# Second layer of the last two blocks of an attention and channel-mixing kernel: four of its seven products grow in one PSUM place, by token halves

## The chip, the cores and the metric

The kernel runs on one core of a Trainium2 chip. The metric is the device time of one execution in microseconds (us). Three runs of the kernel before took 336.69 to 336.91 us, with a median of 336.83 us. The profile shows one further execution, which took 336.81 us; the span from its first to its last instruction is 335.1 us.

The engines are named as in the profile: PE (TensorE, matrix products), DVE (VectorE), ACT (ScalarE), POOL (GpSimd) and SP (SyncE, which here only issues DMAs). The name of an engine with a q behind it (DVEq) is its sequencer, which waits on semaphores, branches and issues DMAs.

## The reference

An attention with extra "beacon" keys, then a token mix of low rank, then two dense layers over channels with a residual:

```python
scores = scale * np.matmul(q, k_all.transpose(0, 1, 3, 2))     # 8 batches, 8 heads, 576 queries, 592 keys, D = 64
a = np.exp(scores - max);  a /= a.sum(-1, keepdims=True) + 1e-09
x = np.matmul(a, v_all)                                        # then heads side by side: 8 x 576 x 512
u = x + (x.transpose(0, 2, 1) @ U @ V).transpose(0, 2, 1)      # token mix, rank 32
out = u + np.maximum(u @ w_ch1, 0.0) @ w_ch2                   # 512 -> 2048 -> 512 channels
```

The inputs and the output are float32. The kernel keeps operands of matrix products in float16 and sums in float32.

## The kernel before

All 4608 rows of the mixed tokens are cut into nine blocks of 512 tokens. Block 0 is computed plainly. Blocks 1 to 8 come from `fast_units`, which returns a list of small units; the main program takes them from one queue, in order, and puts attention work between them while there is any. Engine queues are in order, and the order of the program is kept, so the order of the units is the order on each engine. The last two blocks, 7 and 8 (`QUADS`), run when attention is nearly over; for them `quads` is true, and for block 8 `last` is true as well.

A block's first layer leaves g, the 2048 hidden values of 512 tokens, in the tile gT. The second layer multiplies g by w2 with seven products instead of eight (a scheme of Strassen's kind). g is cut by hidden half and token half into a11, a12 (first 256 tokens) and a21, a22 (last 256); VectorE makes four sums of these (`sums`, line 624):

- S1 = a21 + a22, S2 = S1 - a11, S3 = a11 - a21, S4 = a12 - S2.

The matching combinations of w2 (wt) are made once. The products, with the letter of their PSUM tile:

- M1 = a11 b11 (A), M2 = a12 b21 (F), M6 = S2 t2 (B), M7 = S3 t3 (C), M5 = S1 t1 (D, fresh), M4 = a22 t4 (E), M3 = S4 b22 (D, added to M5).

The four quarters of the output, each 256 tokens by 256 channels, are then

- out11 = M1 + M2, out12 = M1 + M6 + M5 + M3, out21 = M1 + M6 + M7 + M4, out22 = M1 + M6 + M7 + M5,

plus the residual u, which lies token-major in the float16 tile ut. A product is two halves of 128 tokens; a half is 8 matmuls of 256 columns into [128, 256] float32. For the block marked `last`, the second half of D is cut again into two of 128 columns.

Before the change a product's PSUM tile [128, 2, 256] holds both halves, and `after(k)` deals with it when both are done. ScalarE copies M1 to SBUF as s1 (line 800). VectorE adds F + s1 (out11), B + s1 (u2 = M1 + M6) and C + u2 (u3), each 128x512 (line 782). In blocks 7 and 8 GpSimd adds the residual to u2 for out12 before the D sums are there, and in block 8 also to u3 for out22; out11 and out21 get theirs from GpSimd after VectorE's add (`residual`). In block 8 the order is A, F, B, C, E, D, D, since lines 842 and 843 swap M4 ahead of M5; in block 7 it is A, F, B, C, D, E, D. `after_g` (line 746) says after which unit a piece of a sum is issued to VectorE.

`store` issues the DMA to HBM. In block 7 a store is put on SP's queue a few units later. In block 8 it is issued at once: out11 and out21 whole (256 KB) on SP, out22 whole on ACT, out12 in three pieces (128 KB and 64 KB on SP, 64 KB on ACT).

The end of the program is a conditional: a register says whether the general version has to run, which it does not on these inputs. The register is loaded 12 units before the end, a hint for the branch (line 1508 in the profile) stands 5 units before the end, and each engine reaches the branch (line 1463) when its last unit has been issued. Behind the branch an engine has a few semaphore instructions, and SP then waits for every DMA and every engine; a barrier over the engines closes the program. All sequencers read their instructions from memory, with DMAs that the profile calls kind instruction.

Of the kernel before, what the change touches and what calls it, by code (L numbers as in the profile page):

```python
# [11 lines left out]
F32 = mybir.dt.float32  # L12
I32 = mybir.dt.int32
AF = mybir.ActivationFunctionType
# [4 lines left out]
P = 128  # L19
# [11 lines left out]
def kernel(  # L31
# [13 lines left out]
    nc = tc.nc  # L45
    B, H, S, D = q.shape
# [5 lines left out]
    NDC = FF // P  # L52
    NH2 = H // 2
    E = D + 1
# [45 lines left out]
    small = ctx.enter_context(tc.tile_pool(name="small", bufs=2))  # L100
# [70 lines left out]
    HF, HC, HT = NDC // 2, DM // 2, 256  # L171
# [423 lines left out]
    def fast_units(t0, dst, last=False, quads=False):  # L595
# [21 lines left out]
        def sums(i, d0, n):  # L617
            a11, a12, a21, a22 = cell["a"]
            s1, s2, s3, s4 = cell["s"]
            o, x, y, op = [  # L620
                (s1, a21, a22, ALU.add), (s2, s1, a11, ALU.subtract),
                (s3, a11, a21, ALU.subtract), (s4, a12, s2, ALU.subtract),
            ][i]
            nc.vector.tensor_tensor(out=o[:, ds(d0, n)], in0=x[:, ds(d0, n)], in1=y[:, ds(d0, n)], op=op)  # L624
# [118 lines left out]

            return [lambda k=k, slot=slot: unit(k, slot) for k, slot in enumerate(slots)]

        after_g = {0: ((0, 6, 2), (1, 6, 2)), 1: ((2, 0, 4),), 2: ((2, 4, 4),), 7: ((3, 0, 4),), 8: ((3, 4, 4),)}
        sums_at = after_g if quads else {k - NDC: x for k, x in SUMS.items()}

        b11, b21, b22 = w2[:, 0:HF, 0:HC], w2[:, HF:NDC, 0:HC], w2[:, HF:NDC, HC:DM]
        t1, t2, t3, t4 = (wt[:, i, :, :] for i in range(4))  # L750

        def pieces(bank):
            return [(0, 0, HC), (1, 0, P), (1, P, P)] if last and bank == "D" else [(0, 0, HC), (1, 0, HC)]

        def product(bank, a, bm, fresh, i, c0, w):
            key = (bank, i, c0) if last and bank == "D" else bank
            if key not in banks:
                banks[key] = pst([P, w] if key != bank else [P, 2, HC], F32, name="mps" + bank)
            ps = banks[key] if key != bank else banks[key][:, i, :]
            for d in range(HF):  # L760
                nc.tensor.matmul(  # L761
                    ps, a()[:, d, ds(P * i, P)], bm[:, d, ds(c0, w)],
                    start=fresh and d == 0 and (i == 0 or key != bank), stop=d == HF - 1, skip_group_check=True,
                )

        def freed(bank):
            for key in [k for k in banks if k == bank or k[0] == bank]:
                emptying(banks.pop(key))
# [12 lines left out]
        def add(out, x, y, eng=nc.vector):  # L781
            eng.tensor_tensor(out=out, in0=x, in1=y, op=ALU.add)  # L782

        def store(name, h, c, i=None, c0=0, w=HC):
            if i is None:
                both = dst(2 * h, 2 * P)[:, ds(HC * c, HC)].rearrange("(k p) c -> p k c", p=P)
                eng = nc.scalar if last and name == "22" else nc.sync
                u = lambda t=obs[name]: eng.dma_start(out=both, in_=t)
                storing.append([2, u]) if not last else u()
            else:  # L790
                eng = nc.scalar if i and not c0 else nc.sync
                eng.dma_start(out=dst(2 * h + i, P)[:, ds(HC * c + c0, w)], in_=obs[name][:, i, ds(c0, w)])

        def residual(name, h, c):
            add(obs[name], obs[name], u_of(h, c), nc.gpsimd)
            store(name, h, c)

        def after(k):
            if k == 0:
                nc.scalar.activation(out=kept("s1"), in_=banks["A"], func=AF.Copy)  # L800
                freed("A")
            elif k == 1:
                add(out_tile("11"), banks["F"], cell["s1"])
                freed("F")
                residual("11", 0, 0)
            elif k == 2:
                add(kept("u2"), banks["B"], cell["s1"])
                freed("B")
                if quads:
                    add(out_tile("12"), cell["u2"], u_of(0, 1), nc.gpsimd)  # L810
            elif k == 3:
                add(kept("u3"), banks["C"], cell["u2"])
                freed("C")
                if last:
                    add(out_tile("22"), cell["u3"], u_of(1, 1), nc.gpsimd)
            elif products[k][0] == "E":
# [3 lines left out]
            elif products[k][3] and not last:  # L820
                add(out_tile("22"), banks["D"], cell["u3"])
                residual("22", 1, 1)
            elif not last:
                add(obs["12"] if quads else out_tile("12"), banks["D"], obs["12"] if quads else cell["u2"])
                freed("D")
                if quads:
                    store("12", 0, 1)
                else:
                    residual("12", 0, 1)

        def a_of(i):
            return lambda: cell["a"][i]
# [9 lines left out]
        if last:  # L842
            products[4:6] = products[5:3:-1]

        def c_unit(k, j):
            bank = products[k][0]
            p = pieces(bank)[j]
            product(*products[k], *p)
            late = quads and k == 3
            for x in () if late else sums_at.get(2 * k + j, ()):  # L850
                sums(*x)
            if bank == "D" and last:
                i, c0, w = p
                o = obs["22" if products[k][3] else "12"][:, i, ds(c0, w)]
                add(o, banks["D", i, c0], o)
                if k == 6:
                    store("12", 0, 1, i, c0, w)
                    emptying(banks.pop(("D", i, c0)))
                elif j == len(pieces(bank)) - 1:
                    store("22", 1, 1)  # L860
            elif j == len(pieces(bank)) - 1:
                after(k)
            for x in sums_at.get(2 * k + j, ()) if late else ():
                sums(*x)

        units = g_quads() if quads else [lambda k=k: g_unit(k) for k in range(NDC)]
# [157 lines left out]
    first = []  # L1024
# [488 lines left out]
```

## Time and profile before

| what | value |
|---|---|
| median of 3 runs | 336.83 us (336.69 to 336.91) |
| the profiled execution, whole | 336.81 us |
| its span | 335.1 us |
| PE busy, share of the span | 326.1 us, 97% |
| DVE, ACT, POOL busy | 249.8, 190.5, 156.2 us |
| mean granted PE clock | 0.997 of full speed |
| second layer of block 7 on PE | from 291.75 us on |
| second layer of block 8 on PE | from 316.80 us on |
| last compute instruction | DVE, from 329.62 us on |

A page's numbers are those of one execution. A line of the timeline names its start, its length, engine, line of the code, operation, output and inputs by the program's names, shape and count, and in brackets the idle time before it and what ended it. Times of PE rows are of pipelined matmuls whose ends are modelled: rows of neighbouring products overlap a little, so the pace is read from one row's end to the next one's.

### The profile page before, as it was taken

Reading aid. Unit: us, or ns where it says so; the run is one execution under the profiler, and the core shown is the slowest. Engines: PE = TensorE matmul, PEld = TensorE weight load, DVE = VectorE, ACT = ScalarE, POOL = GpSimd, SP = SyncE. Lnnn points to the kernel's source line nnn. Section 1 sums busy time; section 2 is a strip of 40 time slices with the busy share of each in tenths; the row PEclk is TensorE's granted clock in tenths of the full one; section 3 lists DMA queues with packets and bytes.
Section 4 is the critical chain, followed back from the end, with each engine's and each line's share of the span. In section 5 each row is a group of like instructions: output and inputs, shape, how many; then the busy total and the mean of one; then the engine's idle time right before and its main releaser. Section 6 shows DMA issues by size and latency. Waiting matters only on the chain.

```text
span 335.1 us, 9084 instructions
## 1 busy us (share of the span) xinstructions
PE 326.1 (97%) x3614; PEld 223.5 (67%) x3614; DVE 249.8 (75%) x564; ACT 190.5 (57%) x411; POOL 156.2 (47%) x191
## 2 busy tenths in 40 slices
PE   8899999999999999999999999999999999999992
PEld 3565655555577656865687888755875588788792
DVE  6676888678897768765876677677777978786782
ACT  5957951788973677167735784469445404604600
POOL 8988815764336540687067805160497014022041
PEclk9999999999999999999999999999999999999998
DMA  7999999999999994999999997974113514104113
GB/s 158 149 180 166 177 205 188 206 185 140 67 149 146 132 179 80 147 183 170 162 101 182 149 126 115 123 157 87 51 33 103 86 43 125 33 32 129 30 35 103
DMA packets 150530, 41.99 MB, mean 125 GB/s; under 512 B 131280, under 2 KB 149904, under 8 KB 150480
## 3 DMA queue, kind: packets, MB, share of 16 engines
q0 software_dynamic: 87568, 18.18, 71.9%
q1 hardware_dynamic: 62272, 22.54, 37.1%
q8 instruction: 30, 0.49, 0.6%
q10 hardware_dynamic: 640, 0.62, 0.6%
q14 instruction: 20, 0.16, 0.2%
HBM read 37.45 MB, written 9.44 MB: 140 GB/s over the span
## 4 chain that ended last, share of the span: by engine, by line
PE 89%; DVE 3%; POOL 2%; ACT 2%; DMA 2%; issue 1%; DVEq 0%; POOLq 0%
PE gps L635 24%; PE po L427 9%; PE mpsD L761 8%; PE sps L409 6%; PE mpsF L761 4%; PE cps L913 4%; PE mpsC L761 4%; PE mpsB L761 4%; PE mpsA L761 4%; PE gps L887 4%; PE mpsE L761 4%; PE qpsA L674 3%; PE gps L663 2%; DMA vs<-in_v_dram 2%; PE qpsD L674 2%; PE sps L370 1%
## 5 line engine op out<-in xcount | busy, mean ns | idle before, releaser
L418 ACT ACTIVATE expt<-sps 128x496 f16<-128x496 f32 (+2 forms) x192 | 82.1, 544 | 41.6 <-PE sps L409 41.6
L782 POOL TENSOR_TENSOR ob<-ob,ut 128x512 f32<-128x512 f32 x29 | 35.1, 1211 | 129.3 <-DVE ob L782 120.5
L761 PEld LDWEIGHTS <-gT 128*128 128x128 f16 x912 | 85.4, 98 | 13.4 <-issue 3.1
L635 PE MATMUL gps<-uT,w 128*128 128x512 f16 (+1 forms) x448 | 91.9, 349 | 0.2 <-ACT kT L1039 0.2
L635 PEld LDWEIGHTS <-w 128*128 128x128 f16 x448 | 40.4, 98 | 31.9 <-issue 2.5
L646 ACT ACTIVATE gT<-gps 128x512 f16<-128x512 f32 x72 | 42.8, 617 | 25.2 <-PE gps L635 19.9
L624 DVE TENSOR_TENSOR gT<-gT 128x1024 f16<-128x1024 f16 (+3 forms) x90 | 46.7, 542 | 1.0
L240 POOL DMA_DIRECT2D vs<-in_v_dram x50 | 39.7, 807 | 13.1 <-DMA w<-in_moe_w_ch_dram 10.7
L427 PEld LDWEIGHTS <-expt 128*128 128x128 f16 x900 | 33.8, 98 | 10.0 <-issue 1.8
L427 PE MATMUL po<-vs,expt 128*128 128x65 f16 x900 | 36.5, 194 | 0.4 <-DMA vs<-in_v_dram 0.2
L348 DVE TENSOR_TENSOR expt<-expt,bigmask 128x768 f16<-128x768 f16 x54 | 35.3, 694 | 1.4 <-ACT expt L418 1.2
L436 DVE TENSOR_TENSOR xb<-po,rec 128x320 f16<-128x320 f32 x64 | 31.5, 492 | 2.2
L435 DVE RECIPROCAL rec<-po 128x5 f32<-128x5 f32 x64 | 12.1, 189 | 19.4 <-PE po L427 19.0
L644 DVE TENSOR_SCALAR gT<-gps 128x512 f16<-128x512 f32 x24 | 16.5, 689 | 13.0 <-PE gps L635 12.4
L686 ACT ACTIVATE lk<-qpsA 128x512 f32<-128x512 f32 x18 | 10.3, 598 | 25.3 <-PE qpsA L674 25.3
L409 PE MATMUL sps<-qT,kT 64*128 64x80 f16 (+4 forms) x288 | 22.6, 281 | 0.0
L376 ACT ACTIVATE expt<-sps 128x496 f16<-128x496 f32 (+2 forms) x48 | 20.4, 565 | 0.6 <-PE sps L370 0.6
L986 POOL DMA_DIRECT2D st<-in_q_dram x20 | 17.0, 870 | 7.4 <-DMA qT<-st 6.9
L409 PEld LDWEIGHTS <-kT 64*128 64x128 f16 x288 | 10.2, 94 | 12.8 <-issue 8.2
L986 POOL DMA_DIRECT2D st<-in_k_dram x20 | 16.9, 856 | 1.6 <-DMA st<-in_q_dram 1.6
L761 PE MATMUL mpsE<-wt,gT 128*128 128x256 f16 x128 | 16.3, 273 | 0.0
L887 PE MATMUL gps<-uT,w 128*128 128x512 f16 x64 | 16.2, 379 | 0.1
(145 smaller groups left out, 463.5 us busy)
## 6 DMA issues: line engine op xcount, KB each, us to landing
out_dram<-ob SPq DMA_DIRECT2D x34, 256.0 KB, 3.0
vs<-in_v_dram POOLq DMA_DIRECT2D x18, 128.0 KB, 6.7
w<-in_moe_w_ch_dram POOLq DMA_DIRECT2D x4, 512.0 KB, 6.3
w<-in_moe_w_ch_dram POOLq DMA_DIRECT2D x2, 1024.0 KB, 12.8
st<-in_k_dram POOLq DMA_DIRECT2D x12, 128.0 KB, 6.6
st<-in_q_dram POOLq DMA_DIRECT2D x12, 128.0 KB, 7.1
st<-in_k_dram POOLq DMA_DIRECT2D x4, 288.0 KB, 11.8
st<-in_q_dram POOLq DMA_DIRECT2D x4, 288.0 KB, 12.7
```

Source lines behind the costliest of these rows:

```text
L240: nc.gpsimd.dma_start(out=dst[a : a + nq[j], j, :, :], in_=src[hs, ds(q0[j], nq[j]), :].rearrange("h p d -> p h d"))
L348: nc.vector.tensor_tensor(out=e, in0=e, in1=bigmask[:, :, :].rearrange("p (a b) x -> p a b x", b=2), op=ALU.min)
L409: nc.tensor.matmul(banks[i][:, ds(at0 + o, w)], kT(hp, c, ch), qT[hp, c, ds(qa, w)], start=True, stop=True, skip_group_check=len(unit) > 1,)
L418: nc.scalar.activation(out=at[p][3][i][:, ds(AT[g], gw[g])], in_=bank[:, ds(at0, gw[g])], func=AF.Exp, scale=scale)
L427: nc.tensor.matmul(po[:, j, :], ex[0 : nk[c], ds(blk[(c, j)], P)], vs[0 : nk[c], ds(c * H * E + h * E, E)], start=(c == 0), stop=(c == j),)
L436: nc.vector.tensor_tensor(out=xb[:, :, ds(h * D, D)], in0=po[:, :, 0:D], in1=r.broadcast_to([P, NT, D]), op=ALU.mult)
L624: nc.vector.tensor_tensor(out=o[:, ds(d0, n)], in0=x[:, ds(d0, n)], in1=y[:, ds(d0, n)], op=op)
L635: nc.tensor.matmul(g[:, ds(o, w)], w1[:, cc, ts(dc, P)], uT[:, cc, ds(at, w)], start=(cc == 0 and o == 0), stop=(cc == NCC - 1), skip_grou ...
L646: nc.scalar.activation(out=cell["g"][:, dc, :], in_=g, func=AF.Relu)
L761: nc.tensor.matmul(ps, a()[:, d, ds(P * i, P)], bm[:, d, ds(c0, w)], start=fresh and d == 0 and (i == 0 or key != bank), stop=d == HF - 1, ...
L782: eng.tensor_tensor(out=out, in0=x, in1=y, op=ALU.add)
L986: coming.append(lambda d=dst, s=src, a=m[j] - nq[j], n=m[j], j=j: nc.gpsimd.dma_start(out=d[a:n, j, :, :], in_=s[:, ds(q0[j], nq[j]), :].r ...
```

## The change

It concerns blocks 7 and 8 alone. A new function `chain_units` replaces `c_unit` there:

- M1, M6, M7 and M4 are accumulated into the same PSUM tile, one tile of [128, 256] for each token half (name "A"). Between two of them the tile is read: ScalarE copies half by half after M1 (s1, for out11), VectorE adds it to the residual after M6 (out12), after M7 (out22) and after M4 (out21). VectorE thus reads ut itself, and the tiles u2 and u3 are gone, and with them GpSimd's adds for out12, out22 and out21. Only out11 keeps GpSimd's.
- The order in both blocks is A, F, B, D, C, E, D (M1, M2, M6, M5, M7, M4, M3). M5 has its own tiles, by half (and in block 8 by three pieces, as before). VectorE adds M5 to out22 right after M7's half, and M5 + M3 to out12 at the end.
- The pieces of S3 and S4 are issued at other units: the second half of S3 after the first half of M6 instead of before M2, the two of S4 after the first two pieces of M5.
- In block 8 out22 and out21 are stored by halves of 128 KB: out22's first half on SP and its second on ACT, out21's both on ACT. In block 7 stores are as before.

The numbers of units (14 for block 7, 16 for block 8) are the same, so that the branch hint and the register's load stand at the same unit counts.

```diff
-        after_g = {0: ((0, 6, 2), (1, 6, 2)), 1: ((2, 0, 4),), 2: ((2, 4, 4),), 7: ((3, 0, 4),), 8: ((3, 4, 4),)}
-        sums_at = after_g if quads else {k - NDC: x for k, x in SUMS.items()}
+        after_g = {0: ((0, 6, 2), (1, 6, 2)), 1: ((2, 0, 4),), 4: ((2, 4, 4),), 6: ((3, 0, 4),), 7: ((3, 4, 4),)}
+        sums_at = {k - NDC: x for k, x in SUMS.items()}
...
-                eng = nc.scalar if i and not c0 else nc.sync
+                eng = nc.scalar if name == "21" or i and not c0 else nc.sync
                 eng.dma_start(out=dst(2 * h + i, P)[:, ds(HC * c + c0, w)], in_=obs[name][:, i, ds(c0, w)])
...
-        if last:
-            products[4:6] = products[5:3:-1]
...
+        def chain_units():
+
+            halves = [(0, 0, HC), (1, 0, HC)]
+            small = [(0, 0, HC), (1, 0, P), (1, P, P)] if last else halves
+
+            def grown(k, name, i, c0, w):
+                _, a, bm, _ = products[k]
+                fresh = (name, i, c0) not in banks
+                if fresh:
+                    banks[name, i, c0] = pst([P, w], F32, name="mps" + name)
+                ps = banks[name, i, c0]
+                for d in range(HF):
+                    nc.tensor.matmul(
+                        ps, a()[:, d, ds(P * i, P)], bm[:, d, ds(c0, w)],
+                        start=fresh and d == 0, stop=d == HF - 1, skip_group_check=True,
+                    )
+                return ps
+
+            def first(i, c0, w):
+                ps = grown(0, "A", i, c0, w)
+                if i == 0:
+                    kept("s1")
+                nc.scalar.activation(out=cell["s1"][:, i, :], in_=ps, func=AF.Copy)
+
+            def second(i, c0, w):
+                product(*products[1], i, c0, w)
+                if i:
+                    after(1)
+
+            def begun(k, name, h, c, i, c0, w):
+                ps = grown(k, "A", i, c0, w)
+                if i == 0:
+                    out_tile(name)
+                add(obs[name][:, i, :], ps, u_of(h, c)[:, i, :])
+
+            def ended(name, i, c0, w):
+                o = obs[name][:, i, ds(c0, w)]
                 add(o, banks["D", i, c0], o)
...
+            def sent(name, h, c, i, c0, w):
+                if last:
+                    store(name, h, c, i, c0, w)
+                elif i:
+                    store(name, h, c)
+
+            def third(i, c0, w):
+                begun(3, "22", 1, 1, i, c0, w)
+                for p in small:
+                    if p[0] == i:
+                        ended("22", *p)
+                sent("22", 1, 1, i, c0, w)
+
+            def fourth(i, c0, w):
+                begun(5, "21", 1, 0, i, c0, w)
+                sent("21", 1, 0, i, c0, w)
+                freed(("A", i, c0))
+
+            def fifth(*p):
+                grown(6, "D", *p)
+                ended("12", *p)
+                sent("12", 0, 1, *p)
+                freed(("D", p[0], p[1]))
+
+            steps = [(first, halves), (second, halves), (lambda *p: begun(2, "12", 0, 1, *p), halves)]
+            steps += [(lambda *p: grown(4, "D", *p), small), (third, halves), (fourth, halves), (fifth, small)]
+            us = [lambda f=f, p=p: f(*p) for f, ps in steps for p in ps]
+
+            def unit(n, u):
+                u()
+                for x in after_g.get(n, ()):
+                    sums(*x)
+
+            return [lambda n=n, u=u: unit(n, u) for n, u in enumerate(us)]
+
+        if quads:
+            return g_quads() + chain_units()
```

More of the change, by code (lines that the diff above doesn't have):

```diff
@@ L819, in after @@
                 residual("21", 1, 0)
[L820 to L824, printed above, removed]
+            else:
+                add(out_tile("12"), banks["D"], cell["u2"])
                 freed("D")
[L826 to L829, printed above, removed]
+                residual("12", 0, 1)
         def a_of(i):
@@ L848, in c_unit @@
             product(*products[k], *p)
-            late = quads and k == 3
-            for x in () if late else sums_at.get(2 * k + j, ()):
+            for x in sums_at.get(2 * k + j, ()):
                 sums(*x)
-            if bank == "D" and last:
-                i, c0, w = p
-                o = obs["22" if products[k][3] else "12"][:, i, ds(c0, w)]
-                add(o, banks["D", i, c0], o)
[L856 to L862, printed above, removed]
```

32 lines of the change are left out of this document (14 added, 18 removed).

## The prediction

> **What bounds the kernel now.** I read the page first, for where time can be lost at all.
>
> ```profile
> span 335.1 us, 9084 instructions
> ## 1 busy us (share of the span) xinstructions
> PE 326.1 (97%) x3614; PEld 223.5 (67%) x3614; DVE 249.8 (75%) x564; ACT 190.5 (57%) x411; POOL 156.2 (47%) x191
> ```
>
> TensorE is busy for 97% of the span and the change leaves it the same matmuls, so only its gaps and the stretch behind its last matmul can move. Next, the chain in order of time, of which these are the first and last of the seven products of block 7:
>
> ```profile
> 291.75 1.75 PE mpsA L761 x16
> ...
> 302.43 1.75 PE mpsD L761 x16
> ```
>
> From 291.75 to 302.43 + 1.75 = 304.18 us stand seven products at 1.75 us and one tiny matmul: no gap, nothing to win in block 7, something to lose. Then the timelines of TensorE, VectorE and GpSimd for block 8:
>
> ```profile
> 321.87 1.91 PE L761 MATMUL mpsC<-wt,gT 128*128 128x256 f16 x16
> 323.62 1.91 PE L761 MATMUL mpsE<-wt,gT 128*128 128x256 f16 x16
> 325.37 1.93 PE L761 MATMUL mpsD<-wt,gT 128*128 128x256 f16 x24
> 327.65 1.93 PE L761 MATMUL mpsD<-w,gT 128*128 128x256 f16 x24 [0.36 <-DVE ob L782]
> ```
>
> ```profile
> 321.32 0.68 DVE L782 TENSOR_TENSOR ob<-mpsF,kept 128x512 f32<-128x512 f32 x1
> 322.07 0.69 DVE L782 TENSOR_TENSOR kept<-mpsB,kept 128x512 f32<-128x512 f32 x1
> 323.82 0.69 DVE L782 TENSOR_TENSOR kept<-mpsC,kept 128x512 f32<-128x512 f32 x1 [1.05 <-PE mpsC L761]
> 324.43 2.24 DVE L624 TENSOR_TENSOR gT<-gT 128x1024 f16<-128x1024 f16 x2
> 326.59 0.68 DVE L782 TENSOR_TENSOR ob<-mpsE,kept 128x512 f32<-128x512 f32 x1
> 327.19 0.80 DVE L782 TENSOR_TENSOR ob<-mpsD,ob 128x256 f32<-128x256 f32 x3
> 328.73 0.74 DVE L782 TENSOR_TENSOR ob<-mpsD,ob 128x256 f32<-128x256 f32 x2 [0.73 <-PE mpsD L761]
> 329.62 0.29 DVE L782 TENSOR_TENSOR ob<-mpsD,ob 128x128 f32<-128x128 f32 x1 [0.15 <-PE mpsD L761]
> ```
>
> ```profile
> 322.13 1.16 POOL L782 TENSOR_TENSOR ob<-ob,ut 128x512 f32<-128x512 f32 x1 [17.69 <-DVE ob L782]
> 323.25 1.16 POOL L782 TENSOR_TENSOR ob<-kept,ut 128x512 f32<-128x512 f32 x1
> 324.64 1.48 POOL L782 TENSOR_TENSOR ob<-kept,ut 128x512 f32<-128x512 f32 x1 [0.23 <-POOL ob L782]
> 327.35 1.15 POOL L782 TENSOR_TENSOR ob<-ob,ut 128x512 f32<-128x512 f32 x1 [1.23 <-DVE ob L782]
> ```
>
> TensorE has one gap in block 8, 0.36 us ahead of M3. M3 grows in the tile that VectorE must first read for out22, and VectorE comes late: its two sums of S4 take 2.24 us together, beside GpSimd's add at 324.64. Alone they cost 0.7 us each:
>
> ```profile
> L624 DVE TENSOR_TENSOR gT<-gT 128x1024 f16<-128x1024 f16 x2 | 1.3, 685 | 0.0
> ```
>
> The last arithmetic ends at 329.62 + 0.29 = 329.91 us, and the span at 335.1: 5.2 us of tail. The busy times by stretch (the last two columns are the DMA engines' busy share and GB/s) and the issues (KB each, us to landing; the last row is the last store) tell what it is:
>
> ```profile
> 329.00:330.00 1.00, 0.58 (x11) 0.41 (x8) 0.74 (x3) 0.00 (x0) 0.00 (x0) 1.00 0.99 325
> 330.00:331.00 1.00, 0.00 (x0) 0.00 (x0) 0.00 (x0) 0.00 (x0) 0.00 (x0) 1.00 1.04 334
> 331.00:332.00 1.00, 0.00 (x0) 0.00 (x0) 0.00 (x0) 0.00 (x0) 0.00 (x0) 1.00 0.57 139
> 332.00:333.00 1.00, 0.00 (x0) 0.00 (x0) 0.00 (x0) 0.00 (x0) 0.00 (x0) 1.00 0.19 40
> ```
>
> ```profile
> out_dram<-ob SPq DMA_DIRECT2D x1, 64.0 KB, 3.9
> ```
>
> From 329 us the DMA engines are full for two and a half microseconds. out22 (ready at about 328), out21 (ready when GpSimd ends, 327.35 + 1.15 = 328.5) and out12 go out together, 768 KB; at 330 GB/s that is 2.3 us. The last 64 KB land 3.9 us after their issue, at about 333.8. A 256 KB store with nothing beside it, the one issued at 323.3, needs:
>
> ```profile
> DMA to landing us min/median/max: 2.2/2.2/2.2
> ```
>
> A second thing ends as late. These are the branch at the end and the first instruction behind it, by sequencer:
>
> ```profile
> L1463 POOLq EVENT_SEMAPHORE  x5: 17/42/43, 330.0 to 330.3; - x5
> ...
> L1463 POOLq COMPARE_BRANCH  x1: 63/63/63, 327.4 to 327.4; - x1
> ...
> L1463 DVEq COMPARE_BRANCH  x1: 90/90/90, 329.6 to 329.6; - x1
> L1463 ACTq COMPARE_BRANCH  x1: 68/68/68, 329.9 to 329.9; - x1
> ...
> L1463 ACTq EVENT_SEMAPHORE  x1: 17/17/17, 331.6 to 331.6; - x1
> L1463 DVEq EVENT_SEMAPHORE  x1: 21/21/21, 333.9 to 333.9; - x1
> ```
>
> VectorE's sequencer goes on only at 333.9, 4.3 us after its branch; GpSimd's took 2.6 us (327.4 to 330.0), ScalarE's 1.7. VectorE's instructions seem to be fetched through the same full DMA engines. So two paths reach the end: last landing 333.8 and 1.3 us, or VectorE's resumption 333.9 and 1.2 us.
>
> **The change, part by part.**
>
> *TensorE's order.* A half is 1.75 / 2 = 0.87 us. C ends at 321.87 + 1.91 = 323.78, so A ended at 318.53, F at 320.28, B at 322.03. In the new order M5 ends at 323.78, M7's halves at 324.66 and 325.53, M4's at 326.40 and 327.28, M3 at 327.28 + 1.93 = 329.21, if TensorE never waits: 0.36 us earlier than 329.58.
>
> *VectorE, step by step.* M2's add (0.68) stands behind one sum of S3 less, so it starts at 320.7 instead of 321.3 and GpSimd's residual of out11 runs from about 321.5 to 322.7. A 128x256 add costs
>
> ```profile
> L782 DVE TENSOR_TENSOR ob<-mpsD,ob 128x256 f32<-128x256 f32 x2 | 0.8, 416 | 0.7 <-PE mpsD L761 0.7
> ```
>
> 0.42 us. M6's first half is read 321.33 to 321.75. Then comes the moved half of S3, while GpSimd runs. The pair at 324.43 shows the price: it ended at 326.67, 0.55 after GpSimd's add (324.64 + 1.48 = 326.12). So I let S3 wait for GpSimd and end at 322.7 + 0.55 = 323.25; without that it would be 322.4. M7 begins at 323.78: cover 0.5 us. M6's second half is read by 323.7, and the two sums of S4, with GpSimd idle, at 0.6 us from start to start, end at about 324.9. M7's first half (324.66) is read 324.9 to 325.3 and M5 added to it by 325.7; M4's first half may enter that tile from 325.53, cover 0.2 us. M7's second half is read 325.7 to 326.1, M4's second half needs it at 326.40, cover 0.3. M3 needs M5's tiles read by 325.7 (first half) at 327.28: where 0.36 us were lost, 1.5 are spare. M4's adds follow at 326.7 and 327.3, M3's at 328.2, 328.6 and 329.26, the last 0.29 long: VectorE ends at 329.55 against 329.91, so **-0.36 us**. The covers of 0.2 and 0.3 are thin; beyond them each 0.1 us of VectorE's lateness is 0.1 us of TensorE's. Nothing excludes 0.5 us there; I take none, as every duration in the list is a measured one.
>
> *GpSimd* loses three adds (1.16, 1.48, 1.15): off the path by themselves. *ScalarE* copies M1 by halves, with 1.75 us of M2 as cover. It issues out22's second half and both of out21, behind which only its 64 KB of out12 wait: the issues fall at about 326.6, 326.9 and 327.8, that of out12 at 328.9. SP issues out22's first half at 325.6, then out12 at 328.65 and 329.58.
>
> *Block 7.* The same order has covers of 0.6 us (S3 before M7) and some 0.3 us (M4 into M7's tile). No gap there before, none expected: 0.
>
> *The stores.* out22 goes out 1.5 to 2.5 us earlier, out21 about 1 to 1.5. Behind 328.6 us only out12's 256 KB are left, 0.8 us at 330 GB/s, and the last 64 KB are issued when the 128 before them are nearly through. Landing after issue: from 2.2 (the lone 256 KB) to 3.9 (today); I take 2.4, near the lone row since the queue in front is gone. The Trainium skill, "DMA: Bandwidth & Descriptors", section "Latency and other measured facts", gives 0.2 us on average and 2 us at high load for an access to HBM, the largest part of a DMA's fixed cost; by that alone the whole excess of 1.7 us would be load and the time 0.2 lower.
>
> *VectorE's sequencer.* Branch at 329.6 - 0.36 = 329.25. From branch to going on: 1.7 (ScalarE's row) to 4.3 (its own, DMA engines full). GpSimd's 2.6 was with them nearly idle; I take 3.0, close to that, for a third of the traffic.
>
> **Sum.** By the landing: 329.58 + 2.4 + 1.3 = 333.3. By VectorE's sequencer: 329.25 + 3.0 + 1.2 = 333.45. The later decides: a span of 333.4, and with 336.81 - 335.1 = 1.7 around it **335.1 us**, 1.7 us or 0.5% under the profiled 336.81 (which is 0.02 under the median). Lower end: landing 1.6 (below 2.2, for a quarter of its bytes) gives 332.5, ScalarE's 1.7 gives 332.15, so 334.1. Upper end of this case, with 3.9 in the landing's place or a stall of 0.5: 335.9.
>
> **Rivals.**
>
> 1. *The tail is not the stores' load.* VectorE's sequencer takes its 4.3 us whatever else moves. Then 329.25 + 4.3 + 1.2 = 334.75, and **336.4 us**: the same within 0.2%, about what a measurement of this kernel can tell from no change. For it: GpSimd's fetch was slow with idle engines too. Against: ScalarE's and GpSimd's were both far shorter.
> 2. *A code fetch sits in front of the last store.* In 330.3 to 330.6 us one instruction packet kept a DMA engine:
>
> ```profile
> q8 instruction: 1, 0.02, 23.2%
> ```
>
> 23.2% of 16 engines for 0.3 us is 1.1 us of one. A store waits for its slowest engine: 2.2 + 1.1 = 3.3 us, end 329.58 + 3.3 + 1.3 = 334.2, **335.9 us**. For it: after 332 us the DMA engines still work at a share of 0.19, a few stragglers. The Trainium skill, same page, section "Queues, rings and completion order", says each DMA engine takes turns between queues by whole packets, so a packet of code holds up the data behind it; the straggling share agrees.
> 3. *Slower: in-place growth ties TensorE to VectorE.* Each of M6, M7 and M4 must wait, half by half, until the tile is read. There are 3 x 2 x 2 = 12 such handovers; were each fully exposed at 0.42 us, TensorE would lose 5.0 us, **340.2**; with half of them 337.6. It decides once more than four are exposed (1.7 / 0.42). For it: covers of 0.2 to 0.3 us in four of them a block at most. Against: the halves alternate, and between M1, M6 and M7 stands a product of 1.75 us.
>
> **How the numbers follow.** The likeliest case, 335.1 (334.1 to 335.9), has 0.60, and 0.04 lies below it. Rival 2 has 0.15, rival 1 has 0.13, rival 3 has 0.08. Faster by over 0.2% (below 336.16): 0.60 + 0.04 + 0.15 = 0.79; within 0.2%: 0.13; slower: 0.08. The range reaches to rival 1: 334.1 to 336.5, leaving 0.04 below and 0.08 above.
>
> **What would show it.** Right: no idle time before M3; the 128x1024 sums of S4 at 0.7 us; DVE's last add 0.3 to 0.4 us earlier than 329.91; the DMA share under 0.9 from 330 us on, the last store landing in 2.2 to 3 us, VectorE's first instruction behind the branch before 333. Wrong: TensorE waiting for VectorE at mpsA's third or fourth product, in block 7 above all; a last landing still near 3.9; or a resumption of VectorE 4 us behind its branch, which would leave little more than the 0.36.

## The result, and the profile after

The changed kernel takes **335.65 us** (median of 8 runs, 335.21 to 336.39) against 336.76 us (336.39 to 337.13, 8 runs) of the kernel before, run beside it: a ratio of **0.9968, 95% interval 0.9957 to 0.998**. It is faster by 1.1 us or 0.3%. The forecast was 335.1 (334.1 to 336.5). The profiled execution took 336.39 us with a span of 334.5 us. It is the slowest of the eight, 0.74 us above their median, so the profile shows less gain than the median.

The head of the page, to set beside that of before:

```profile
span 334.5 us, 9085 instructions
PE 326.3 (98%) x3614; PEld 223.9 (67%) x3614; DVE 251.7 (75%) x572; ACT 190.8 (57%) x413; POOL 148.5 (44%) x185
```

The timelines of TensorE, VectorE and GpSimd in block 8 (start, length, engine, line, operation; in brackets the idle time before it):

```profile
316.90 1.91 PE L854 MATMUL mpsA<-w,gT 128*128 128x256 f16 x16
...
323.90 3.66 PE L854 MATMUL mpsA<-wt,gT 128*128 128x256 f16 x32
327.40 1.93 PE L854 MATMUL mpsD<-w,gT 128*128 128x256 f16 x24
```

```profile
321.60 0.42 DVE L780 TENSOR_TENSOR ob<-mpsA,ut 128x256 f32<-128x256 f32 x1
321.94 1.50 DVE L624 TENSOR_TENSOR gT<-gT 128x1024 f16<-128x1024 f16 x1
323.37 0.41 DVE L780 TENSOR_TENSOR ob<-mpsA,ut 128x256 f32<-128x256 f32 x1
323.70 1.28 DVE L624 TENSOR_TENSOR gT<-gT 128x1024 f16<-128x1024 f16 x2
324.98 0.42 DVE L780 TENSOR_TENSOR ob<-mpsA,ut 128x256 f32<-128x256 f32 x1
...
326.72 0.42 DVE L780 TENSOR_TENSOR ob<-mpsA,ut 128x256 f32<-128x256 f32 x1
327.60 0.42 DVE L780 TENSOR_TENSOR ob<-mpsA,ut 128x256 f32<-128x256 f32 x1 [0.45 <-PE mpsA L854]
...
329.36 0.29 DVE L780 TENSOR_TENSOR ob<-mpsD,ob 128x128 f32<-128x128 f32 x1 [0.15 <-PE mpsD L854]
```

```profile
321.74 1.16 POOL L780 TENSOR_TENSOR ob<-ob,ut 128x512 f32<-128x512 f32 x1 [23.76 <-DVE ob L780]
```

TensorE's row of M3 has no bracket any more: the gap is gone, and no handover of the growing tiles made a new one. VectorE now waits for TensorE and not the other way round (0.45 and 0.15). Block 8 as a whole starts 0.27 us later than before (316.90 against 316.63). So does block 7 (291.85 against 291.58), and so does M3 of block 6 (277.36 against 277.10), whose code is the same in both kernels. (For the kernel before, the table ahead of the prediction has 316.80 and 291.75; these are from the chain, whose pieces begin 0.17 us behind the timeline's rows.) This offset arises upstream of the change. The distances inside block 8 are therefore read from the start of its A: the last add of VectorE ends 12.75 us behind it (329.36 + 0.29 - 316.90), before 13.28 (329.91 - 316.63): 0.53 us gained.

The tail: busy times by stretch (the last two columns are the DMA engines' busy share and GB/s), the stores being issued from 328 us on (KB each, median us to landing; the first row is out21's two halves), and the branch at the program's end by sequencer (ns, then when):

```profile
329.00:330.00 1.00, 0.33 (x6) 0.15 (x3) 0.50 (x2) 0.00 (x0) 0.00 (x0) 1.00 0.56 190
330.00:331.00 1.00, 0.00 (x0) 0.00 (x0) 0.00 (x0) 0.00 (x0) 0.00 (x0) 1.00 0.69 199
331.00:332.00 1.00, 0.00 (x0) 0.00 (x0) 0.00 (x0) 0.00 (x0) 0.00 (x0) 1.00 0.20 33
332.00:333.00 1.00, 0.00 (x0) 0.00 (x0) 0.00 (x0) 0.00 (x0) 0.00 (x0) 1.00 0.07 16
```

```profile
out_dram<-ob ACTq DMA_DIRECT2D x2, 128.0 KB, 3.0
out_dram<-ob SPq DMA_DIRECT2D x1, 128.0 KB, 3.8
out_dram<-ob ACTq DMA_DIRECT2D x1, 64.0 KB, 3.7
out_dram<-ob SPq DMA_DIRECT2D x1, 64.0 KB, 3.4
```

```profile
L1515 POOLq EVENT_SEMAPHORE  x5: 17/43/43, 322.9 to 323.3; - x5
L1515 SPq EVENT_SEMAPHORE  x5: 17/17/17, 332.4 to 332.8; - x5
L1515 POOLq COMPARE_BRANCH  x1: 69/69/69, 322.4 to 322.4; - x1
...
L1515 DVEq COMPARE_BRANCH  x1: 90/90/90, 329.4 to 329.4; - x1
L1515 ACTq COMPARE_BRANCH  x1: 68/68/68, 329.6 to 329.6; - x1
L1515 SPq COMPARE_BRANCH  x1: 78/78/78, 330.1 to 330.1; - x1
L1515 ACTq EVENT_SEMAPHORE  x1: 17/17/17, 330.1 to 330.1; - x1
L1515 DVEq EVENT_SEMAPHORE  x1: 21/21/21, 333.0 to 333.0; - x1
```

The DMA engines are no longer full (0.56 and 0.69 where it was 0.99 and 1.04). Still the last 64 KB need 3.4 us, and VectorE's sequencer goes on 3.6 us after its branch (333.0 - 329.4), before 4.3. In 332 to 333 us the DMA engines are at a share of 0.07: a few stragglers. The span ends 1.5 us behind VectorE's resumption.

What ends this execution is neither the last store nor VectorE. SP's sequencer stands from its branch at 330.1 until 332.4, for the landing of out21's second half, issued at 328.15:

```profile
L789 ACTq DMA_DIRECT2D out_dram<-ob x1: 388/388/388, 328.1 to 328.1; - x1
...
DMA to landing us min/median/max: 4.3/4.3/4.3
```

```profile
L1560 SPq EVENT_SEMAPHORE  x14: 17/28/28, 332.8 to 334.4; - x14
L1560 SPq DRAIN  x3: 7/7/13, 333.6 to 333.9; - x3
```

From 332.42 on SP goes through its five and then twelve semaphore instructions, one every 60 to 100 ns, until 333.6; the barrier takes the other 0.9 us. When it comes to VectorE and to the last store (landed at 333.06), both are through already. The trace records a store's completion in sixteen parts: fifteen of this one were in at 329.92, and the sixteenth came at 332.41.

### The profile page after: what moved, and what is told of

The parts are those of the page before. It is cut to its first block, busy times and chain, and to the rows that moved or that the text cites. A ratio compares the mean times of both kernels' runs of the same rounds, so it can differ in the third digit from the quotient of the medians.

```text
span 334.5 us, 9085 instructions
## 1 busy us (share of the span) xinstructions
PE 326.3 (98%) x3614; PEld 223.9 (67%) x3614; DVE 251.7 (75%) x572; ACT 190.8 (57%) x413; POOL 148.5 (44%) x185
## 4 chain that ended last, share of the span: by engine, by line
PE 91%; ACT 5%; DVE 1%; issue 0%
PE gps L635 24%; PE po L427 8%; PE mpsD L760 6%; PE sps L409 6%; PE mpsF L760 4%; PE cps L965 4%; PE mpsA L854 4%; PE gps L939 4%; PE mpsE L760 3%; PE qpsA L674 3%; PE mpsC L760 3%; PE mpsA L760 3%; PE mpsB L760 3%; ACT expt L376 2%; PE mpsD L854 2%; PE gps L663 2%
## 5 line engine op out<-in xcount | busy, mean ns | idle before, releaser
L780 POOL TENSOR_TENSOR ob<-ob,ut 128x512 f32<-128x512 f32 x26 | 31.3, 1207 | 131.2 <-DVE ob L780 121.5
L624 DVE TENSOR_TENSOR gT<-gT 128x1024 f16<-128x1024 f16 (+3 forms) x90 | 47.5, 550 | 1.0
L348 DVE TENSOR_TENSOR expt<-expt,bigmask 128x768 f16<-128x768 f16 x54 | 34.4, 676 | 1.4 <-ACT expt L418 1.2
```

Source lines behind the costliest of these rows:

```text
L348: nc.vector.tensor_tensor(out=e, in0=e, in1=bigmask[:, :, :].rearrange("p (a b) x -> p a b x", b=2), op=ALU.min)
```

## The experiments

The theory that the runs were chosen to test: the tail is the stores' queue plus the code that the sequencers fetch behind the closing branch, on the same DMA engines; the gain hangs on stores that leave earlier. The rivals: that the gain is TensorE's alone, or that the tail belongs to the branch whatever the stores do. Ratios are to the kernel before, run on the same chip.

**Both kernels without the closing branch.** The general version goes, and with it the register's load, the hint and the branch:

```diff
-        n_bad = nc.values_load(badi[0:1, 0:1], min_val=0, max_val=P)
-        fill(len(queue) - HINT)
-        with tc.block():
-            tc.mark_branch_hint_location("general", engines=[ENG.PE, ENG.Activation, ENG.DVE, ENG.SP, ENG.Pool])
-            fill(len(queue))
+        fill(len(queue))
...
-    with tc.If(n_bad != 0, label="general"):
...
```

> The kernel before without the conditional at its end: the general version, the load of its register and the branch hint are left out. Theory A (the tail is the load of the stores: 768 KB in front of the last landing): the last store still lands 3.9 us after its issue, only the resumption of the sequencers goes, so the time stays within 0.3 us of 336.8. Theory B (code fetched after the branch holds a DMA engine, and the stragglers on it make the last landing late): without the branch the 768 KB drain in 2.3 us from 329.1 on, the last landing comes about 2 us after its issue, at about 331.9, and the time falls by 1.5 to 2 us, to about 335.0.

> The changed kernel without the conditional at its end (general version, register load and hint left out). Theory A: the change has already emptied the queue in front of the last store, so little is left to win: 0.3 us under the changed kernel's 335.65. Theory B: the last store lands 1.6 to 2.2 us after its issue instead of 3.4, and VectorE need not resume behind a branch: 1.0 to 1.5 us under 335.65, about 334.4. The difference between this and the kernel before without the conditional is then what the change is worth without the fetch: 0.5 us of TensorE's wait plus the stores' load, 0.5 to 0.9 us.

Measured: 335.14 us for the kernel before without it (335.05 to 335.74, 5 runs, ratio 0.9952, 0.9939 to 0.9965) and 334.1 for the changed one (333.99 to 334.49, 5 runs, 0.992, 0.9907 to 0.9933), the kernel before standing at 336.9 on that chip. The branch, with all that belongs to it, is worth 1.76 us in the kernel before (336.9 - 335.14) and 1.55 in the changed one (335.65 - 334.1, from two comparisons), and the change 1.04 us without it (335.14 - 334.1) as against 1.1 with it. Landings of all stores from 322 us on, without the branch, of before and then of the changed kernel:

```profile
DMA to landing us min/median/max: 2.0/2.2/2.6
```

```profile
DMA to landing us min/median/max: 1.7/1.8/2.2
```

Even with full DMA engines (a share of 1.01 from 330 to 331 us in the kernel before without the branch) the last store lands 2.0 us after its issue, not 3.9. So the larger part of the late landings comes with the branch, not with the load. The sixteen parts say how: without the branch those of the last store come within 0.2 us of each other in the kernel before (331.85 to 332.05); with it twelve are in by 331.89, and the last comes at 333.79. From 322 us on the profile of the kernel before has two packets of 16 KB and seven of 8 KB of kind instruction, and without the branch one of 8 KB. The change's gain, by the medians, doesn't depend on the branch.

**The stores whole again, in the new order.**

```diff
-                u = lambda t=obs[name]: nc.sync.dma_start(out=both, in_=t)
+                eng = nc.scalar if last and name == "22" else nc.sync
+                u = lambda t=obs[name]: eng.dma_start(out=both, in_=t)
...
             def sent(name, h, c, i, c0, w):
-                if last:
+                if last and name == "12":
```

> The changed kernel with one part undone: in block 8 out22 and out21 are stored whole, out22 on ACT and out21 on SP as before the change, when their second half is ready. Theory A: 128 KB of out22 and 128 KB of out21 move about 0.9 us later, the backlog in front of out12 grows by 256 KB less what has drained, 0.3 to 0.5 us slower than 335.65. Theory B: the held DMA engine has 8 more packets of 46 ns to drain, 0.2 to 0.4 us. If the halves do not matter: 335.65.

Measured: 335.96 us (335.7 to 336.25, 7 runs), ratio 0.9976 (0.9965 to 0.9987). By the medians the halves are worth some 0.3 us, but the intervals overlap, so that they are worth anything isn't shown.

**The gap closed in the old order.** In the kernel before S4's sums go ahead of M2's add, so that M3 finds its tile free:

```diff
-        after_g = {0: ((0, 6, 2), (1, 6, 2)), 1: ((2, 0, 4),), 2: ((2, 4, 4),), 7: ((3, 0, 4),), 8: ((3, 4, 4),)}
+        after_g = {0: ((0, 6, 2), (1, 6, 2)), 1: ((2, 0, 4), (2, 4, 4)), 2: ((3, 0, 4),), 3: ((3, 4, 4),)}
```

> The kernel before with one edit: the two sums of S4 go to VectorE ahead of M2's add instead of behind u3, where GpSimd's adds stood in their way. If TensorE's wait before M3 in block 8 comes from those late sums, it goes from 0.36 us to under 0.1, the last VectorE add ends 0.4 to 0.5 us earlier, and the time is 336.3. If another wait takes its place (GpSimd's residual of out22 comes later, since out11 is later by 1.2 us), 336.7 and the wait stays.

Measured: 336.7 us (12 runs), ratio 1.0003 (0.9984 to 1.0021). The gap is gone, and no gain is shown: the medians are 0.2 us apart (336.9 before on that chip), and the interval, wide by one run of 340.18 us, would hold a gain of 0.5 us. TensorE's M3, VectorE's last add and VectorE's sequencer at the branch:

```profile
327.23 1.93 PE L761 MATMUL mpsD<-w,gT 128*128 128x256 f16 x24
```

```profile
329.19 0.29 DVE L782 TENSOR_TENSOR ob<-mpsD,ob 128x128 f32<-128x128 f32 x1 [0.15 <-PE mpsD L761]
```

```profile
L1463 DVEq COMPARE_BRANCH  x1: 90/90/90, 329.2 to 329.2; - x1
...
L1463 DVEq EVENT_SEMAPHORE  x1: 21/21/21, 333.9 to 333.9; - x1
```

The last add ends at 329.48, 0.43 us earlier than before, and VectorE goes on at 333.9 as before, now 4.7 us behind its branch. In this execution the tail absorbs what TensorE gains. out22 and out21 also left 0.4 and 0.7 us earlier than before, and out11 1.2 us later, so the run isn't TensorE's gain alone. It does show that the gap closes without tiles that grow: the place of S4's sums is enough.

**The new order with late stores.** out21 and then out22 whole, on SP, when out21 is ready:

```diff
             def sent(name, h, c, i, c0, w):
-                if last:
+                if last and name == "12":
                     store(name, h, c, i, c0, w)
-                elif i:
+                elif i and not (last and name == "22"):
                     store(name, h, c)
+                    if last:
+                        store("22", 1, 1)
```

> The changed kernel, but in block 8 out21 is stored whole on SP and out22 whole on SP behind it, so that both leave at 328.1 to 328.6 us, as late as before the change; TensorE's and VectorE's work is untouched. If the gain came from the stores' earlier start, it falls back to that of TensorE's wait alone, which in the run with the early S4 sums was worth nothing: 336.5 to 336.8. If the gain is TensorE's 0.5 us and the order of the stores does not matter: 335.7 to 336.0.

Measured: 336.44 us (12 runs), ratio 0.9988 (0.9967 to 1.0009). TensorE keeps its gain (last add from 329.40, block 8's A from 316.93), and the kernel loses most of its own: 0.3 us is left by the medians (336.73 before on that chip). Its stores from 328 us on, and its branch:

```profile
out_dram<-ob SPq DMA_DIRECT2D x2, 256.0 KB, 4.3
out_dram<-ob SPq DMA_DIRECT2D x1, 128.0 KB, 4.2
out_dram<-ob ACTq DMA_DIRECT2D x1, 64.0 KB, 4.1
out_dram<-ob SPq DMA_DIRECT2D x1, 64.0 KB, 3.8
```

```profile
L1517 DVEq COMPARE_BRANCH  x1: 90/90/90, 329.4 to 329.4; - x1
...
L1517 DVEq EVENT_SEMAPHORE  x1: 21/21/21, 333.6 to 333.6; - x1
```

With the queue back, VectorE's resumption is back at 4.2 us. So it follows the stores, and the forecast's first rival, in which it takes 4.3 whatever else moves, falls.

**The chain in block 8 alone.** Block 7 gets the old order, store and adds back (`c_unit` for it, `chain_units` for block 8):

```diff
-        if quads:
+        if last:
             return g_quads() + chain_units()
-        units = [lambda k=k: g_unit(k) for k in range(NDC)]
+        units = g_quads() if quads else [lambda k=k: g_unit(k) for k in range(NDC)]
...
```

> Only block 8 uses the new chain, block 7 keeps its order and its adds on GpSimd. TensorE had no gap in block 7 before or after (25.05 us from the start of block 7's second layer to that of block 8's in both), so the whole effect should be there: 335.65 within 0.3 us, 1.1 us under the kernel before. If block 7 has a share of the effect that the traces do not show, 336.0 or above, or below 335.3.

Measured: 335.73 us (335.44 to 336.56, 12 runs), ratio 0.9965 (0.9946 to 0.9984), as the whole change. That block 7 is worth anything isn't shown.

**TensorE's branch behind the last add.** The packets of 330.2 to 330.4 us in the changed kernel, by queue (packets, MB, share of 16 engines), have one of 16 KB that holds a DMA engine for about a microsecond (30.0% of 16 engines for 0.2 us):

```profile
q8 instruction: 1, 0.02, 30.0%
```

Were it TensorE's fetch, and were that alone the trouble, a TensorE that branches later would leave the last store free. VectorE copies a column of out12's last piece, and a matmul of one column reads it:

```diff
+    def hold_pe(o):
+        nc.vector.tensor_copy(out=warm, in_=o)
+        hps = pst([1, 1], F32, name="hps")
+        nc.tensor.matmul(hps, warm, ones, start=True, stop=True)
+        emptying(hps)
...
                 freed(("D", p[0], p[1]))
+                if last and p == small[-1]:
+                    hold_pe(obs["12"][:, 1, HC - 1 : HC])
```

> The changed kernel with one thing added: VectorE copies one column of the last out12 piece to a small tile and TensorE multiplies it by ones, unused, so that TensorE's sequencer reaches the branch only after the last add, at 329.8 instead of 328.1 us. Theory B (the code that TensorE fetches 2.1 us behind its branch holds one DMA engine, with the stores' last packets behind it): the 16 KB packet moves from 330.2 to about 331.9, behind the data; the last store lands about 2 us after its issue instead of 3.4 and VectorE goes on earlier than 333: 0.6 to 1.2 us faster than the changed kernel, 334.5 to 335.0. Rival theory C (VectorE's and the others' fetches hold the engine, TensorE's is innocent, or the engine is held as long wherever the fetch stands): 335.65 or up to 0.7 us slower, since TensorE itself goes on later.

> The same addition in the kernel before. Theory B: TensorE's branch moves from 328.3 to about 330.1 us, its packet to 332.1, by when the 768 KB have drained (without the branch the last landing was at 332.05): the last landing falls from 333.8 to about 332.3, 0.8 to 1.3 us faster than before, 335.5 to 336.0. Theory C: 336.8 or slower.

Measured: 336.2 us (335.88 to 337.1, 12 runs), ratio 0.9977 (0.9958 to 0.9995) in the changed kernel, and 337.6 (336.6 to 337.97, 12 runs), 1.0013 (0.9994 to 1.0032) in the one before. No gain in either. The stores from 328 us on in the changed kernel so edited:

```profile
out_dram<-ob ACTq DMA_DIRECT2D x2, 128.0 KB, 2.3
out_dram<-ob SPq DMA_DIRECT2D x1, 128.0 KB, 1.9
out_dram<-ob ACTq DMA_DIRECT2D x1, 64.0 KB, 1.8
out_dram<-ob SPq DMA_DIRECT2D x1, 64.0 KB, 3.6
```

The stores ahead of the fetches now land in 1.8 to 2.3 us, as without a branch; three of these four had needed 3.7 to 4.3 in the changed kernel. So the fetches do seem to hold stores up. But the last one still needs 3.6 us: four instruction packets begin between 331.6 and 332.1 us, with this store in flight, and fifteen of its parts are in at 332.06, the sixteenth at 333.99. That a later TensorE leaves the last store free is refuted. Whose packet holds which DMA engine, TensorE's or another's, isn't in the profile, and stays open.

**The hint's place, out21's queue, and the changed kernel once more.**

```diff
-    HINT = 5
+    HINT = 12
```

```diff
-    HINT = 5
+    HINT = 2
```

```diff
-                eng = nc.scalar if name == "21" or i and not c0 else nc.sync
+                eng = nc.scalar if i and not c0 else nc.sync
```

> The changed kernel with the hint for the closing branch 12 units before the end instead of 5, so about 5 us earlier. Theory (what ends the program is code that each sequencer fetches behind the branch, on the stores' DMA engines): if what the hint fetched stays until the branch is taken, part of the fetch leaves the stretch behind 328 us, VectorE's sequencer goes on by 332.3 and the time is 334.9 to 335.3 us. Rival (the fetch happens at the branch itself, the hint only pays for a part, or an early one is lost again): VectorE's sequencer goes on at 333 as in the changed kernel or later, 335.65 to 336.5 us.

> The changed kernel with the hint 2 units before the end instead of 5, so about 1.7 us later, at about 329 us. Theory (fetches behind the branch): less lead for the fetch, VectorE's sequencer goes on 0.3 to 1 us later than 333.0 and the time is 335.9 to 336.6 us; out21's halves, whose issue the hint held up on ScalarE's queue, leave at about 327.3 and 328.0. Rival (the hint's own fetch collides with out21's stores and is what holds them): they land earlier, and 335.0 to 335.5 us.

> The changed kernel with out21's first half on SP's queue instead of ScalarE's, so that it leaves when VectorE has written it, at about 327.1 instead of 327.7, and the second on ScalarE at about 328.0. Theory (the backlog in the DMA engines behind 328 us plus code): at most 0.1 us earlier last landing, 335.4 to 335.7 us. Rival (ScalarE's queue is what holds the tail up, since the branch of ScalarE stands behind its stores): out21 lands 0.5 us earlier and the time is 335.0 to 335.3 us.

> The changed kernel once more, on the chip of these three for their comparison: 335.65 us within 0.3, 0.9968 of the kernel before within 0.0015 by all theories.

| kernel | median us (runs) | ratio to before, 95% |
|---|---|---|
| hint 12 units before the end | 335.49 (9) | 0.996 (0.9946 to 0.9974) |
| hint 2 units before the end | 335.95 (8) | 0.9978 (0.9958 to 0.9998) |
| out21 on two queues | 335.15 (6) | 0.9957 (0.9935 to 0.9979) |
| the changed kernel again | 335.78 (6) | 0.996 (0.9946 to 0.9974) |

All four intervals overlap; the hint's place decides nothing that these runs can tell. The early hint's 335.49 lies between the two forecasts made for it (up to 335.3, and from 335.65). The late hint's 335.95 fits the theory's time but not its sign: VectorE went on at 332.8, not later than 333.0. VectorE's sequencer with the early hint, and with out21 on two queues:

```profile
L1515 DVEq COMPARE_BRANCH  x1: 90/90/90, 328.9 to 328.9; - x1
L1515 DVEq EVENT_SEMAPHORE  x1: 21/21/21, 332.1 to 332.1; - x1
```

```profile
L1515 DVEq COMPARE_BRANCH  x1: 90/90/90, 329.0 to 329.0; - x1
L1515 DVEq EVENT_SEMAPHORE  x1: 21/21/21, 332.3 to 332.3; - x1
```

With the early hint VectorE goes on at 332.1, which the theory asked for (by 332.3), but only because block 8's A began at 316.38, half a microsecond earlier than in the changed kernel's profile; from the branch it is 3.2 us. The same holds for out21 on two queues (A at 316.54). There the first half leaves at 326.8 us, the second at 327.7 (in the changed kernel 327.7 and 328.1), and the last two stores land in 2.6 and 2.7 us. It has the lowest median of all kernels with the branch, in the range of its rival (335.0 to 335.3), by which ScalarE's queue holds the tail up. That it beats the change isn't shown: its interval holds the change's ratio.

All kernels with the branch side by side, from their rows of the closing branch, of the last store and of the page's head (us):

| kernel | VectorE's branch | goes on | between | last store, issue to landing | span | span's end behind "goes on" |
|---|---|---|---|---|---|---|
| before | 329.6 | 333.9 | 4.3 | 3.9 | 335.1 | 1.2 |
| before, S4 early | 329.2 | 333.9 | 4.7 | 4.0 | 335.0 | 1.1 |
| before, TensorE late | 329.8 | 334.1 | 4.3 | 3.9 | 335.2 | 1.1 |
| after, late stores | 329.4 | 333.6 | 4.2 | 3.8 | 334.9 | 1.3 |
| after | 329.4 | 333.0 | 3.6 | 3.4 | 334.5 | 1.5 |
| after, again | 329.6 | 332.9 | 3.3 | 3.0 | 334.2 | 1.3 |
| after, TensorE late | 330.4 | 334.2 | 3.8 | 3.6 | 335.3 | 1.1 |
| block 8 alone | 329.5 | 333.1 | 3.6 | 3.2 | 334.3 | 1.2 |
| after, whole stores | 329.5 | 332.8 | 3.3 | 2.7 | 333.9 | 1.1 |
| after, hint early | 328.9 | 332.1 | 3.2 | 3.2 | 333.7 | 1.6 |
| after, hint late | 329.4 | 332.8 | 3.4 | 2.8 | 333.9 | 1.1 |
| after, out21 on two queues | 329.0 | 332.3 | 3.3 | 2.7 | 333.4 | 1.1 |

In each of the twelve the span ends 1.1 to 1.6 us behind VectorE's resumption, but VectorE is not always what SP waits for last. The waits of SP's sequencer from 330 us on tell it (total, times and longest in us), here in the kernel before, with the last store, and with a late hint, with VectorE:

```profile
SPq L1508 <- DMA out_dram<-ob: 0.2, 1, 0.2
```

```profile
SPq L1560 <- DVEq L1515: 0.2, 1, 0.2
```

VectorE decides in the six rows with 1.1 in the last column. In the kernel before and with late stores it is the last store. In the changed kernel, its second run, the chain in block 8 alone and the early hint it is out21's second half; with out21 on two queues that half lands in 1.9 us, and SP has no wait for it.

Where all of the stores go out late, VectorE needs 4.2 to 4.7 us; where out22 leaves early, 3.2 to 3.8. It does not go below 3.2: with out21 on two queues the DMA engines are at a share of 0.18 from 330 to 331 us, and it is still 3.3. An estimate from these rows is that the load sets about one microsecond of it and the branch some three. That the three are the branch's own isn't shown, since no run has VectorE branch with no store in flight.

The Trainium skill, "Runtime: NRT & Kernel Launch", section "Instruction fetch mechanics", says that a taken branch whose target lies outside the two pages of code that an engine holds makes it fetch the target's page by DMA before it can go on. That VectorE stands still for over 3 us behind its branch, and that the program is 1.55 us or more faster without one, agree with it; that what it waits for is such a page isn't shown by a row.

## Why the prediction was right, and where it was off

The direction and the two sources of the gain were right, and the time lies in the range and in that of the likeliest case. The size was off: of 1.7 us came 1.1, and rival 2's 335.9, with a chance of 0.15, is nearer to 335.65 than the forecast's 335.1. The forecast tail was too short by more than TensorE's extra gain made up for, so that the range holds the time says little for the terms of the tail.

**TensorE, -0.36: right in mechanism, too small.** The gain from block 8's A to VectorE's last add is 0.53 us. The step that failed is "M3 at 327.28 + 1.93 = 329.21". 1.93 is the length of a row with a modelled end; the pace of such rows, from one end to the next, is 1.75 or 1.77, as all other steps of the list took it. 329.05 would have been right (329.33 - 0.27 = 329.06, from A). For the same reason an idle time of 0.36 behind an overlapping row was a loss of 0.52: M3 began 11.02 us behind A before (327.65 - 316.63), and 10.50 now.

**VectorE's steps: right.** The moved half of S3 took 1.50 us beside GpSimd's add, and ended at 323.44, or 323.17 without the later start of the block (0.27); forecast 323.25. S4's sums took 1.28 together, against 2.24. M7's first half was read by 325.40, and M4 needed its tile at about 325.65: the cover was 0.25 us, forecast 0.2. The thin covers held, in block 8 and in block 7, where TensorE's rows have no idle time listed, so the slower rival had no place to begin. For S3 the Trainium skill, "SBUF — State Buffer", section "Who interferes with whom", has an exclusive lock: of a VectorE operation with two SBUF inputs and a GpSimd operation that reads SBUF, the one that starts first takes the port that they share, and the other waits until it ends. GpSimd's add started at 321.74, VectorE's sum at 321.94, and the sum took 1.50 us instead of about 0.65, which agrees.

**Block 7, 0: right**, as far as the run with the chain in block 8 alone can tell.

**GpSimd: three adds off the path, right.** Its sequencer now passes the branch at 322.4 and goes on at 322.9, 0.6 us later, where it was 2.6 (with the chain in block 8 alone 2.7, 322.5 to 325.2). So the 2.6 "with them nearly idle", near which VectorE's 3.0 was put, was no fixed price of a fetch.

**The stores: right that they decide, off in size.** "out21 about 1 to 1.5" us earlier was too much: its halves left at 327.7 and 328.1 instead of 326.9 and 327.8, in order on ScalarE's queue. The landing of 2.4 became 3.4 us (3.0 in the second profile). The step took the excess over a lone store for queueing; the runs without the branch show that full DMA engines alone make 2.0 us, and the rest comes with the branch, in single late parts of the stores. That fits rival 2's mechanism, and its 3.3 is nearer to what was measured than 2.4. The Trainium skill's figure for a loaded access to HBM, 2 us at high load in "DMA: Bandwidth & Descriptors", section "Latency and other measured facts", would have put all of the excess down to load; the runs without the branch speak against that.

**VectorE's resumption, 3.0: too short, and not what ended the program.** It measured 3.6 (3.2 to 3.6 over the profiles of the change and of its variants with early stores, 3.8 with TensorE late). The step that failed is that two paths reach the end, the last landing and VectorE's resumption. A third decided the profiled execution: out21's second half, for which the sum has no term ("Behind 328.6 us only out12's 256 KB are left"), landed at 332.41, and SP needed 2.1 us from there (334.5 - 332.4). By VectorE alone the span would have been about 334.1 (332.97 and the 1.1 that stands behind VectorE where it decides), an estimate; the forecast was 333.45. Of the 1.05 us by which this span missed, only 0.55 belong to the median (335.65 - 335.1).

**The sum took gains as additive; with the branch that isn't borne out.** It read the path as TensorE's gain plus the tail's. For neither the gap closed in the old order (1.0003) nor the new order with late stores (0.9988) is a gain shown, as both intervals hold 1; with the earlier end and the earlier stores together it is 0.3%. Without the branch the two do seem to add up: in its profiles the last add starts 0.52 us earlier, counted from block 8's A, the last store lands 0.37 us sooner after its issue (1.65 against 2.02), and the change is worth 1.04 us.

Open: whose packet of code holds which DMA engine; why the old order with S4 early lost at the branch, in its profile, just what TensorE had gained; what the growing tiles are worth against the new order alone, which no run separates; and whether the 0.27 us by which the profiled changed kernel runs late ahead of block 7 is more than a difference between executions (the kernels with the changed code begin block 8 at 316.38 to 317.63, those with the old at 316.50 to 316.72).

## What to carry to other kernels

Read a gap's worth from start to start of the rows around it (11.02 against 10.50 us), not from the idle time listed: rows with modelled ends overlap. Behind the last arithmetic, cost the stores and the code behind a closing branch together: here no gain from an earlier end of the arithmetic could be shown until the stores in front of it left earlier as well. Ask of every store still in flight at the end, not only of the last, whether the closing waits stand behind it. Before shaving tenths off the last products, price the branch itself by leaving it out once: here it was 1.55 to 1.76 us, more than the whole change.

## What the runs showed of the hardware that was not expected

- A conditional at the end that skips the general version, with its hint in place, costs 1.55 to 1.76 us, and moving VectorE's hint from 326.3 to 320.9 or 328.5 us changes nothing that can be told.
- VectorE's sequencer needs 3.2 us and more to go on behind that branch, even with the DMA engines at shares of 0.63, 0.18 and 0.25 in the three microseconds after it (out21 on two queues), and ScalarE's only 0.5 in the changed kernel (329.6 to 330.1).
- Without the branch, 768 KB of stores keep the DMA engines full and the last 64 KB still land 2.0 us after their issue; with it, 512 KB in the same stretch, spread over two microseconds, make it 3.0 to 3.4.
- With the branch one part in sixteen of a store can come 2.5 us behind the other fifteen (329.92 and 332.41 for out21's second half); without it the sixteen parts of the last store come within 0.2 to 0.3 us.
